# A spectral layer and a rational feed-forward block: a turn's transform task and row stage between TensorE's first and second product

## The chip, the cores and the metric

The kernel runs on one core of one Trainium2 chip. The metric is the device time of one execution in microseconds; the time of a kernel is the median of its runs. The engines of the core go through their own instruction streams, each in order, and wait for each other by semaphores: TensorE (PE; its weight loads are listed as PEld), VectorE (DVE), ScalarE (ACT), GpSimd (POOL) and SyncE (SP, which here only issues DMAs).

## The reference

```python
def _attn_ref(x, w_r, w_i, b_r, b_i):          # x: 4 x 3008 x 256
    X = np.fft.rfft(x, axis=1)
    Yr = Xr @ w_r - Xi @ w_i + b_r             # Xr, Xi: real and imaginary part of X
    Yi = Xr @ w_i + Xi @ w_r + b_i
    # soft threshold by 0.01 on both parts
    return np.fft.irfft(Yr + 1j * Yi, n=3008, axis=1)

def _moe_ref(x, w_in, w_out, a, b):            # x: 12032 x 256, w_in: 256 x 2048, w_out: 2048 x 256
    h = x @ w_in
    P = a[0] + a[1] * h + a[2] * h**2 + a[3] * h**3
    Q = 1.0 + abs(b[0]) * abs(h) + abs(b[1]) * h**2
    return (P / (Q + 1e-06)) @ w_out
```

The output of the first function, as 12032 rows, is the input of the second. All of it is float32.

## The kernel before

**Spectral part.** A transform of 3008 points is split in 47 x 64. An image (one of 4 batches) goes through tasks that are Python generators: `f1_task` (8 first-transform tasks, matmuls L195), `f2_task` (12, L255), `m_sum` and `m_rest` (12 each: the mix with w_r and w_i; L297 and L315), `i1_task` (12, the first inverse step, L376). Between them data turn around through DRAM. The tasks of image 0 run in a prologue, those of images 1 to 3 beside the feed-forward part, one or two per turn. The last inverse step is the row stage `i2_task` (L426), which makes the input xsh and xsl of one block of the feed-forward part.

**Feed-forward part.** The 12032 rows are cut in 26 blocks of 470 columns (two blocks have 376). A block goes through 8 units of 256 hidden columns, so there are 208 units. The main loop has one turn per unit i. In turn i TensorE computes the first product of unit i+1 (`g1_mm`, L460, 12 matmuls into the PSUM tile h) and the second product of unit i-3 (`g2_mm`, L553, 12 matmuls into acc). ScalarE reads h of unit i: v and s (L492, L493; step A), t (L499; step a), and for unit i-1 two activations on y (L504, step Y, and the reciprocal root L506, step y). A DMA from GpSimd's queue adds s to v (L497). VectorE computes t of unit i from h (L511, L512), then g of unit i-1 (L520, the high part; it waits for y), then whatever the turn's task left for it, then the low part of g of unit i-2 (L533), then v of unit i-1 (L523). GpSimd does one subtraction (L527). h has two PSUM buffers, so the first product of unit i+1 waits for VectorE's L512 of unit i-1. Blocks of work for the transform tasks take their PSUM from a second pair of buffers, `ft`.

**What sets the order.** The order of a turn is a string of steps, gone through letter by letter (L831):

```python
order = "Fs1AaehmYy2" if i < 4 else "F1AasYehmy2" if storing(i) else "Fs1AaYehmy2"
```

F lets the row stage (in two of eight turns) and the planned tasks issue their matmuls; for `m_sum` it first issues a copy of `offset` into the PSUM bank on ScalarE, `copy(0, pt[:, 0], offset)`, and the L297 matmuls wait for it. The steps 1 and 2 are the two products, s stores a finished block (two copies acc to ob on ScalarE), e and h let the tasks evict their PSUM on ScalarE (L159, L263, L264, L319, L429). VectorE's part of a task (L267, L268, L321, L437) comes after L520. Which tasks stand in which turn is set by a planner with fixed costs (`spent`, `budget`, `plan`), not by time. When no transform task is left (`nextb == B and not cur`), the string is changed: the row stage's second half comes late and another form of the stage is used. In that part of the program, from the turn after the last task, the order is the same in both kernels.

Of the kernel before, what the change touches and what calls it, by code (L numbers as in the profile page):

```python
# [18 lines left out]
B, S, D, DFF = 4, 3008, 256, 2048  # L19
# [82 lines left out]
def spectral_moe(ctx, tc, t, out):  # L102
# [61 lines left out]
    def flush():  # L164
        while late:
            late.pop(0)()
# [246 lines left out]
    def i2_task(n, ec):  # L413
        if ec == 0:
            alone[n] = nextb == B and not cur
            xs_t[n] = (mx.tile([128, 2, TB], F32R, tag="xsh", name="xsh"), mx.tile([128, 2, TB], F32R, tag="xsl", name="xsl"))
        xh, xl = xs_t[n]
        ct = c_t[n]
        w = len(blocks[n]) * TJ
        pt = ps.tile([128, 512], F32, tag="ft", name="pi2")  # L420
        last = len(blocks[n]) - 1
        for i in range(JB):
            z = slice(i * TJ, 512 if i == JB - 1 and not alone[n] else (i + 1) * TJ)
            if i <= last or not alone[n]:
                k = min(i, last)
                nc.tensor.matmul(out=pt[:, z], lhsT=ct[:, k, ec * 128:(ec + 1) * 128], rhs=i2[:, :z.stop - z.start],  # L426
                                 start=i == 0, stop=True, skip_group_check=True)
        yield
        nc.scalar.activation(out=xh[:, ec, :w], in_=pt[:, :w], func=ACTF.Copy)  # L429
        yield  # L430
        if alone[n]:
            nc.tensor.matmul(out=pt[:, :w], lhsT=minus, rhs=xh[:, ec, :w], start=False, stop=True, skip_group_check=True)
            yield
            nc.scalar.activation(out=xl[:, ec, :w], in_=pt[:, :w], func=ACTF.Copy)
        else:
            yield
            nc.vector.tensor_tensor(out=xl[:, ec, :w], in0=pt[:, :w], in1=v32(xh[:, ec, :w]), op=ALU.subtract)  # L437
# [48 lines left out]
    def act_a(u):  # L486
        w = width(u)
        d = un[u]
        h = d["h"][:, :, :w]
        for nm, bufs in (("s", 2), ("v", 4), ("t", 4)):  # L490
            d[nm] = fresh(nm, bufs, u)
        nc.scalar.activation(out=d["v"], in_=h, func=ACTF.Abs, scale=rate["b0"])  # L492
        nc.scalar.activation(out=d["s"], in_=h, func=ACTF.Square, scale=rate["b1"])  # L493
        if u < 2:
            nc.gpsimd.tensor_tensor(out=d["v"], in0=d["v"], in1=d["s"], op=ALU.add)
        else:
            nc.gpsimd.dma_start(out=d["v"], in_=d["s"], accum_op=ALU.add)  # L497
        yield
        nc.scalar.activation(out=d["t"], in_=h, func=ACTF.Identity, scale=rate["a3"], bias=ca[:, 2:3])  # L499

    def act_b(u):
        d = un[u]
        d["y"] = fresh("y", 3, u)
        nc.scalar.activation(out=d["y"], in_=d["v"], func=ACTF.Square, bias=C0)  # L504
        yield
        nc.scalar.activation(out=d["y"], in_=d["y"], func=ACTF.Abs_reciprocal_sqrt)  # L506
# [62 lines left out]
    def fft_tasks(b):  # L569
        turns = (0, 1, 2, 3, 6, 7, 4, 5) if b == 1 else range(8)  # L570
        ts = [(0.95, 2, 2, f1_task(b, c, pos), 0) for pos, c in enumerate(turns)]
        ts += [(0.0, 0, 0, load_first(b), 0)] + [(0.0, 0, 0, iter(()), 0)] * 2
        np_ = NK // 2
        for p in range(np_ + 2):
            if p < np_:
                ts.append((0.86, 1, 1, f2_task(b, p), 1))
            if p == 0:
                ts.append((0.0, 0, 0, iter(()), 0))
            if 1 <= p <= np_:
                ts += [(0.86, 1, 0, m_sum(b, p - 1), 2), (1.56, 0, 1, m_rest(b, p - 1), 0)]  # L580
            if p >= 2:
                ts.append((0.87, 1, 1, i1_task(b, p - 2), 0))
        return ts
# [29 lines left out]
    with tc.manual_schedule():  # L613
# [185 lines left out]
        cur = []  # L799
        nextb = 1  # L800
# [10 lines left out]
        storing = lambda i: i >= 4 and i % UB == 3  # L811
# [8 lines left out]
        for i in range(-1, nu + 4):  # L820
            flush()
            live = []
            parts = []
            freed = 0
            if i == 3:
                copied.append(1)
            if 0 <= i < nu:
                n, q = divmod(i, UB)
            aa = act_a(i) if 0 <= i < nu else iter(())
            ab = act_b(i - 1) if 0 <= i - 1 < nu else iter(())  # L830
            order = "Fs1AaehmYy2" if i < 4 else "F1AasYehmy2" if storing(i) else "Fs1AaYehmy2"  # L831
            for step in order.replace("m", "").replace("2", "2m").replace("1A", "Ao1") if nextb == B and not cur else order:
                if step == "F":
                    if 0 <= i < nu and n + 1 < nb and q in I2Q:
                        g = i2_task(n + 1, I2Q.index(q))
                        next(g)
                        parts.append(g)
                        held += 1
                        freed += 1
                    if not cur and nextb < B and i >= 0:  # L840
                        cur = first if nextb == 1 else fft_tasks(nextb)
                        last = max(next(k for k in range(nb) if blocks[k][-1] >= nextb * NJ) * UB - UB - 1, i + 1)
                        plan = [load(k) for k in range(i, last)]
                        level = (sum(x[0] for x in cur) + sum(plan)) / len(plan)
                        plan = [level - x for x in plan]
                        nextb += 1
                        spent = budget = 0.0
                    if cur:
                        budget += plan.pop(0) if plan else level
                        while cur and spent + cur[0][0] / 2 < budget and held + cur[0][1] <= 2 and not (live and storing(i)):  # L850
                            cost, use, free, g, part = cur.pop(0)
                            next(g, None)
                            (parts if part == 1 else live).append(g)
                            held += use
                            freed += free
                            spent += cost
                            if not cost or part == 2:
                                break
                elif step == "1" and i + 1 < nu:
                    g1_mm(i + 1)  # L860
                elif step == "2":
                    if 0 <= i - 3 < nu:
                        g2_mm(i - 3, (0, 1) if i - 3 >= UB else (1,))
                    if 0 <= i - 2 < UB:
                        g2_mm(i - 2, (0,))
                elif step == "s" and i >= 4 and (i - 4) % UB == UB - 1:
                    store((i - 4) // UB)
                elif step in "Aa":
                    next(aa, None)
                elif step == "o":  # L870
                    for g in owed:
                        drain(g)
                    owed = []
                elif step in "hm":
                    for g in parts:
                        next(g)
                elif step == "e":
                    for g in live:
                        next(g, None)
                    if i == 0:  # L880
                        next(mix)
                elif step in "Yy":
                    next(ab, None)
            prev, db = db, dve_b(i - 1) if 0 <= i - 1 < nu else iter(())
            next(prev, None)
            if 0 <= i < nu and alone.get(n + 1):
                owed, parts = parts, []
            if 0 <= i < nu:
                dve_a(i)
            if i == 0:  # L890
                drain(mix)
            next(prev, None)
            next(db, None)
            for g in live:
                drain(g)
            for g in parts:
                next(g, None)
            drain(prev)
            for g in parts:
                drain(g)  # L900
            next(db, None)
            if i >= nu:
                drain(db)
            held -= freed
            if len(cur) < 8 and 1 < nextb < B and (nextb, 0) not in xin:
                load_x(nextb, 0)
                load_x(nextb, 1)
            if 0 <= i < nu and q == 1 and n + 1 < nb:
                assert not cur or blocks[n + 1][-1] < (nextb - 1) * NJ
                load_c(n + 1)  # L910
# [33 lines left out]
```

## Time and profile before

| | |
|---|---|
| median of 3 runs | 1416.41 us (1415.95 to 1417.36) |
| profiled execution | 1419.05 us |
| its span, first to last instruction | 1417.3 us |
| granted TensorE clock, mean | 0.998 |
| TensorE matmul, weight loads | 98%, 85% of the span |
| VectorE, ScalarE, GpSimd | 91%, 81%, 47% |

Times in the rows below are microseconds from the start of the span. A matmul row is busy from its start to a modelled end, and matmuls are pipelined, so a busy TensorE may stand all the same: the distance between starts tells what a group of matmuls took. In a timeline each row has start, duration, engine, line, operation, output<-inputs, shape and count; in brackets stand the idle time of the engine just before it and what ended it.

### The profile page before, as it was taken

The page shows a single profiled execution, that of the slowest core. Times are in us where ns is not written, and L with a number is a line of the kernel's source. Part 1 is how long each engine was busy: PE and PEld are TensorE (multiplying, and loading weights), DVE is VectorE, ACT ScalarE, POOL GpSimd, SP SyncE. Part 2 cuts the span into 40 slices and gives each one's busy share as a digit, 9 for nine tenths or more (in the row PEclk, how much of TensorE's full clock was granted, in tenths as well). Part 3 has the DMA queues.
Part 4 walks back from the last instruction along what each step waited for, and adds up shares of the span by engine and source line. Part 5 has one row for each costly group of instructions (what it writes and reads, how often), then busy time and mean ns, then how long its engine had stood idle before and what let it go on. Part 6 is the DMA issues. An engine that isn't in the chain of part 4 may idle for free.

```text
span 1417.3 us, 20378 instructions
## 1 busy us (share of the span) xinstructions
PE 1390.0 (98%) x7279; PEld 1210.9 (85%) x7279; DVE 1291.5 (91%) x1304; ACT 1144.5 (81%) x1513; POOL 670.5 (47%) x444
## 2 busy tenths in 40 slices
PE   9998999999999999999999999999999999999997
PEld 4977889998878989898888899998888888888887
DVE  3779899898999989999989999999999999999998
ACT  2768887887888778888888778888888898888985
POOL 0444444444554444454545444444545555555553
PEclk9999999999999999999999999999999999999999
DMA  9966556556776556556687465656555465555543
GB/s 309 379 215 162 117 121 150 110 114 158 160 204 151 116 130 141 117 121 156 148 208 158 98 142 126 127 115 133 108 127 118 97 122 96 112 118 99 117 77 80
DMA packets 95657, 200.48 MB, mean 141 GB/s; under 512 B 10748, under 2 KB 51748, under 8 KB 95556
## 3 DMA queue, kind: packets, MB, share of 16 engines
q0 software_dynamic: 29664, 97.62, 38.0%
q1 hardware_dynamic: 65780, 101.51, 23.2%
q8 instruction: 58, 0.95, 0.3%
q14 instruction: 43, 0.35, 0.1%
q10 hardware_dynamic: 112, 0.05, 0.0%
HBM read 54.61 MB, written 37.49 MB: 65 GB/s over the span
## 4 chain that ended last, share of the span: by engine, by line
PE 72%; DVE 10%; issue 9%; ACT 5%; DMA 4%; SPq 0%; DVEq 0%; ACTq 0%
PE h L460 28%; PE acc L553 27%; PE pi L426 4%; PE pft L315 4%; DVE t L511 3%; DVE v L523 3%; PE pft L376 2%; DMA v<-s 2%; PE pft L297 2%; PE pft L255 2%; PE pft L195 1%; PE pft L178 1%; DVE g L520 1%; ACT t L499 1%; DMA s<-zt 1%
## 5 line engine op out<-in xcount | busy, mean ns | idle before, releaser
L553 PE MATMUL acc<-g,wsp 128*128 128x470 f32 (+1 forms) x2496 | 563.7, 375 | 3.4 <-DVE g L533 3.4
L527 POOL TENSOR_TENSOR t<-t,v 128x940 f32<-128x940 f32 (+1 forms) x206 | 469.7, 2280 | 164.4 <-DVE v L523 143.8
L553 PEld LDWEIGHTS acc<-g,wsp 128*128 128x128 f32 x2496 | 470.0, 190 | 62.8 <-DVE g L533 5.0
L460 PE MATMUL h<-xsh,win 128*128 128x470 f32 (+1 forms) x1664 | 436.9, 384 | 6.0 <-DVE t L512 5.6
L497 POOL DMA_DIRECT2D v<-s x206 | 181.6, 882 | 489.7 <-issue 452.9
L460 PEld LDWEIGHTS h<-xsh,win 128*128 128x128 f32 x1664 | 304.8, 189 | 61.6 <-PE acc L553 9.8
L520 DVE SCALAR_TENSOR_TENSOR g<-t,small,y 128x940 fp32r<-128x940 f32 (+1 forms) x208 | 250.3, 1203 | 45.8 <-ACT y L506 42.6
L492 ACT ACTIVATE v<-h 128x940 f32<-128x940 f32 (+1 forms) x208 | 196.2, 943 | 95.4 <-PE h L460 92.1
L511 DVE TENSOR_TENSOR t<-t,h 128x940 f32<-128x940 f32 (+1 forms) x208 | 231.3, 1112 | 27.3 <-ACT t L499 25.6
L512 DVE SCALAR_TENSOR_TENSOR t<-t,small,h 128x940 f32<-128x940 f32 (+1 forms) x208 | 245.2, 1179 | 7.4
L533 DVE SCALAR_TENSOR_TENSOR g<-t,small,y 128x940 fp32r<-128x940 f32 (+1 forms) x208 | 244.2, 1174 | 0.1
L460 PE MATMUL h<-xsl,win 128*128 128x470 f32 (+1 forms) x832 | 241.4, 371 | 0.0
L523 DVE SCALAR_TENSOR_TENSOR v<-v,g 128x940 f32<-128x940 f32 (+1 forms) x208 | 231.8, 1114 | 0.1
L504 ACT ACTIVATE y<-v 128x940 f32<-128x940 f32 (+1 forms) x208 | 206.1, 991 | 21.4 <-DMA v<-s 21.4
L499 ACT ACTIVATE t<-h,small 128x940 f32<-128x940 f32 (+1 forms) x208 | 216.2, 1039 | 0.0
L506 ACT ACTIVATE y<-y 128x940 f32<-128x940 f32 (+1 forms) x208 | 205.1, 986 | 2.0
L493 ACT ACTIVATE s<-h 128x940 f32<-128x940 f32 (+1 forms) x208 | 195.7, 941 | 0.0
L460 PEld LDWEIGHTS h<-xsl,win 128*128 128x128 f32 x832 | 155.8, 188 | 20.1
L426 PEld LDWEIGHTS pi<-small,ct 96*128 96x128 f32 x516 | 65.2, 192 | 7.9 <-ACT s L493 3.6
L426 PE MATMUL pi<-small,ct 96*128 96x94 f32 (+1 forms) x516 | 66.2, 275 | 3.5 <-DVE x L268 2.9
L159 ACT ACTIVATE pft<-offset 128x256 f32<-128x256 f32 x36 | 14.1, 391 | 57.6 <-DVE yt L321 23.3
L255 PEld LDWEIGHTS pft<-f,bt 128*128 128x128 f32 x288 | 37.3, 191 | 4.9 <-DVE yt L321 1.9
(113 smaller groups left out, 1071.0 us busy)
## 6 DMA issues: line engine op xcount, KB each, us to landing
v<-s POOLq DMA_DIRECT2D x190, 470.0 KB, 4.7
xin<-in_x SPq DMA_DIRECT2D x30, 512.0 KB, 6.4
s<-zt SPq DMA_DIRECT2D x48, 256.0 KB, 3.5
out_t<-ob SPq DMA_DIRECT2D x48, 235.0 KB, 4.5
ct<-s SPq DMA_DIRECT2D x20, 480.0 KB, 5.6
bt<-s SPq DMA_DIRECT2D x36, 256.0 KB, 3.3
y<-yt SPq DMA_DIRECT2D x144, 64.0 KB, 2.3
s<-a SPq DMA_DIRECT2D x46, 192.0 KB, 5.1
```

Source lines behind the costliest of these rows:

```text
L460: nc.tensor.matmul(out=h[:, i, :w], lhsT=l, rhs=r, start=k == 0, stop=k == len(halves) // FU - 1)
L492: nc.scalar.activation(out=d["v"], in_=h, func=ACTF.Abs, scale=rate["b0"])
L499: nc.scalar.activation(out=d["t"], in_=h, func=ACTF.Identity, scale=rate["a3"], bias=ca[:, 2:3])
L504: nc.scalar.activation(out=d["y"], in_=d["v"], func=ACTF.Square, bias=C0)
L506: nc.scalar.activation(out=d["y"], in_=d["y"], func=ACTF.Abs_reciprocal_sqrt)
L511: nc.vector.tensor_tensor(out=tt, in0=tt, in1=h, op=ALU.mult)
L512: nc.vector.scalar_tensor_tensor(out=tt, in0=tt, scalar=ca[:, 1:2], in1=h, op0=ALU.add, op1=ALU.mult)
L520: stt(out=hi, in0=tt, scalar=ca[:, 0:1], in1=y, op0=ALU.add, op1=ALU.mult)
L523: stt(out=v, in0=v, scalar=C0, in1=v32(hi), op0=ALU.add, op1=ALU.mult)
L527: nc.gpsimd.tensor_tensor(out=tt[:, :cut], in0=tt[:, :cut], in1=v[:, :cut], op=ALU.subtract)
L533: stt(out=lo, in0=tt, scalar=ca[:, 0:1], in1=y, op0=ALU.add, op1=ALU.mult)
L553: nc.tensor.matmul(out=acc[n][e][:, :w], lhsT=l, rhs=r, start=begun[n][e] == 1, stop=begun[n][e] == 3 * FU * UB)
```

## The change

The branch for the time without transform tasks becomes explicit, with the same strings as before. In the other branch, from turn 4 on, F comes behind 1, A and a (and behind the store's s where there is one to store: `1AaFs`).

```diff
-            order = "Fs1AaehmYy2" if i < 4 else "F1AasYehmy2" if storing(i) else "Fs1AaYehmy2"
-            for step in order.replace("m", "").replace("2", "2m").replace("1A", "Ao1") if nextb == B and not cur else order:
+            if nextb == B and not cur:
+                order = "FAo1asYehy2m" if storing(i) else "FsAo1aYehy2m"
+            else:
+                order = "Fs1AaehmYy2" if i < 4 else "1AaFsYehmy2" if storing(i) else "s1AaFYehmy2"
+            for step in order:
```

TensorE, a turn beside the transforms of the first image there; L255 is an f2 task, L460 the first product, L553 the second (before):

```order
L553 MATMUL acc_1256<-g,wsp_774 128x470 x4
L255 MATMUL pft<-f_70,bt 128x2x64 x4
L460 MATMUL h<-xsh,win_594 128x470 x4
L460 MATMUL h<-xsl,win_594 128x470 x2
L460 MATMUL h<-xsh,win_594 128x470 x4
L460 MATMUL h<-xsl,win_594 128x470 x2
L553 MATMUL acc_1255<-g,wsp_774 128x470 x2
```

and the same place now:

```order
L553 MATMUL acc_1256<-g,wsp_774 128x470 x4
L460 MATMUL h<-xsh,win_594 128x470 x4
L460 MATMUL h<-xsl,win_594 128x470 x2
L460 MATMUL h<-xsh,win_594 128x470 x4
L460 MATMUL h<-xsl,win_594 128x470 x2
L255 MATMUL pft<-f_70,bt 128x2x64 x4
L553 MATMUL acc_1255<-g,wsp_774 128x470 x2
```

The task's matmuls have moved over the 12 matmuls of the first product and stand right before the second.

ScalarE, a turn with `m_sum` (the row `pft<-offset` is the offset copy, `pft<-pft` the eviction step of `m_sum`; before):

```order
L506 ACTIVATE y<-y 128x940
L159 ACTIVATE pft<-offset 128x256
L492 ACTIVATE v<-h 128x940
L493 ACTIVATE s<-h 128x940
L499 ACTIVATE t<-h,small 128x940
L504 ACTIVATE y<-v 128x940
L159 ACTIVATE pft<-pft 128x256
L506 ACTIVATE y<-y 128x940
```

and now:

```order
L506 ACTIVATE y<-y 128x940
L492 ACTIVATE v<-h 128x940
L493 ACTIVATE s<-h 128x940
L499 ACTIVATE t<-h,small 128x940
L159 ACTIVATE pft<-offset 128x256
L504 ACTIVATE y<-v 128x940
L159 ACTIVATE pft<-pft 128x256
L506 ACTIVATE y<-y 128x940
```

The offset copy has moved behind t; the evictions of the tasks stay where they were, in front of L506.

TensorE, the last turn with a transform task (a row stage L426 and an i1 task L376) and the first turn without, whose own row stage is the second L426 (before):

```order
L553 MATMUL acc_9424<-g,wsp_774 128x470 x2
L426 MATMUL pi_9502<-small,ct 128x94 x4
L426 MATMUL pi_9502<-small,ct 128x136
L376 MATMUL pft<-y,g_71 128x256 x2
L460 MATMUL h<-xsh,win_621 128x470 x4
L460 MATMUL h<-xsl,win_621 128x470 x2
L460 MATMUL h<-xsh,win_621 128x470 x4
L460 MATMUL h<-xsl,win_621 128x470 x2
L553 MATMUL acc_9423<-g,wsp_801 128x470 x4
```

and now:

```order
L553 MATMUL acc_9424<-g,wsp_774 128x470 x2
L460 MATMUL h<-xsh,win_621 128x470 x4
L460 MATMUL h<-xsl,win_621 128x470 x2
L460 MATMUL h<-xsh,win_621 128x470 x4
L460 MATMUL h<-xsl,win_621 128x470 x2
L426 MATMUL pi_9522<-small,ct 128x94 x4
L426 MATMUL pi_9522<-small,ct 128x136
L376 MATMUL pft<-y,g_71 128x256 x2
L553 MATMUL acc_9423<-g,wsp_801 128x470 x4
```

Row stage and task now follow the first product of that turn; the next turn's row stage still precedes its first product. VectorE's, GpSimd's and SyncE's instructions stand in the same order in both kernels.

## Rows read from the trace of the kernel before

**Rows 1.** Windows: stretch and length; busy us (count) by engine, clock, DMA.

```profile
core 0: us, PE busy (x) PEld busy (x) DVE busy (x) ACT busy (x) POOL busy (x), PEclk, DMA share, GB/s
143.00:1045.00 902.00, 895.54 (x4749) 791.71 (x4748) 827.60 (x820) 740.85 (x995) 421.97 (x273) 1.00 0.62 137
1045.00:1400.00 355.00, 351.62 (x1719) 309.47 (x1719) 351.51 (x325) 312.47 (x371) 198.59 (x131) 1.00 0.54 107
```

**Rows 2.** Waits, 143 to 1045 us: who <- for whom: total, times, longest.

```profile
ACT v L492 <- PE h L460: 62.5, 80, 1.3
DVE g L520 <- ACT y L506: 41.6, 58, 3.5
DVE t L511 <- ACT t L499: 24.5, 33, 1.1
ACT pft L159 <- DVE yt L321: 23.3, 12, 2.4
```

**Rows 3.** Timeline, a turn with an f2 task and `m_sum`.

```profile
805.00 1.20 PE L460 MATMUL h<-xsh,win 128*128 128x470 f32 x4
...
808.74 0.39 ACT L159 ACTIVATE pft<-offset 128x256 f32<-128x256 f32 x1 [1.87 <-DVE yt L321]
...
811.20 1.03 PE L297 MATMUL pft<-wr,total 128*128 128x256 f32 x4
...
811.88 1.21 PE L460 MATMUL h<-xsh,win 128*128 128x470 f32 x4
...
812.53 0.39 ACT L159 ACTIVATE pft<-pft 128x256 f32<-128x256 f32 x1
812.84 0.39 ACT L263 ACTIVATE total<-pft 128x256 f32<-128x256 f32 x1
...
813.57 1.01 ACT L506 ACTIVATE y<-y 128x940 f32<-128x940 f32 x1
...
814.61 1.20 DVE L520 SCALAR_TENSOR_TENSOR g<-t,small,y 128x940 fp32r<-128x940 f32 x1 [0.45 <-ACT y L506]
...
815.73 0.41 DVE L267 TENSOR_TENSOR total<-pft,total 128x256 f32<-128x256 f32 x1
...
816.66 1.19 DVE L533 SCALAR_TENSOR_TENSOR g<-t,small,y 128x940 fp32r<-128x940 f32 x1
```

**Rows 4.** Timeline, turns without a task: TensorE, then VectorE from one v to the next.

```profile
1050.32 1.02 PE L460 MATMUL h<-xsh,win 128*128 128x470 f32 x4
...
1052.90 2.72 PE L553 MATMUL acc<-g,wsp 128*128 128x470 f32 x12
...
1055.46 1.02 PE L460 MATMUL h<-xsh,win 128*128 128x470 f32 x4
...
1061.15 1.13 DVE L523 SCALAR_TENSOR_TENSOR v<-v,g 128x940 f32<-128x940 f32 x1
...
1066.69 1.13 DVE L523 SCALAR_TENSOR_TENSOR v<-v,g 128x940 f32<-128x940 f32 x1
```

**Rows 5.** Timeline, a turn with row stage and mixed product: its end, evictions, VectorE's part.

```profile
784.53 1.01 PE L460 MATMUL h<-xsh,win 128*128 128x470 f32 x4
784.73 0.60 ACT L319 ACTIVATE yt<-pft 128x512 f32<-128x512 f32 x1 [1.87 <-PE pft L315]
...
785.23 0.56 ACT L429 ACTIVATE xsh<-pi 128x470 fp32r<-128x470 f32 x1
...
785.67 0.99 ACT L506 ACTIVATE y<-y 128x940 f32<-128x940 f32 x1
...
787.81 0.68 DVE L321 SCALAR_TENSOR_TENSOR yt<-pft,yt 128x512 f32<-128x512 f32 x1
...
788.41 0.64 DVE L437 TENSOR_TENSOR xsl<-pi,xsh 128x470 fp32r<-128x470 f32 x1
```

**Rows 6.** Timeline, the same turn on TensorE: first product before it, and its row stage.

```profile
774.67 1.21 PE L460 MATMUL h<-xsh,win 128*128 128x470 f32 x4
...
781.79 1.36 PE L426 MATMUL pi<-small,ct 96*128 96x94 f32 x10 [1.61 <-DVE x L268]
```

**Rows 7.** Timeline, the last turn with a transform task.

```profile
1036.95 1.29 PE L426 MATMUL pi<-small,ct 96*128 96x94 f32 x10
...
1038.76 1.20 PE L460 MATMUL h<-xsh,win 128*128 128x470 f32 x4
...
1041.10 1.20 DVE L520 SCALAR_TENSOR_TENSOR g<-t,small,y 128x940 fp32r<-128x940 f32 x1 [1.34 <-ACT y L506]
```

## The prediction

> **What bounds the kernel now.** I read the busy sums by stretch first, then the waits, then one turn as a timeline. From 143 to 1045 us, the stretch beside transforms, two engines are nearly full: TensorE's matmul rows cover 895.5 of 902 us and VectorE's 827.6 (ScalarE's 740.9), at a granted clock of 1.00, the 2.4 GHz level. From 1045 us on, with no transforms left, VectorE is busy 351.5 of 355 us and nothing else matters [rows 1]. A busy TensorE row can hide a stall, so I went by starts. In a turn without a task the first product starts at 1050.32 us, the second at 1052.90 and the next first product at 1055.46: 2.58 + 2.56 = 5.14 us for 24 matmuls [rows 4]. The turn with an f2 task and a "sum" task lasts from 805.00 to 811.88 = 6.88 us, and the two tasks alone account for the 1.74 us over 5.14 [rows 3]. Turns of the same make-up repeat that length, so beside transforms TensorE issues without pause and sets the pace, except in six places named below. VectorE and ScalarE wait there for each other: 24.5 us for t, 23.3 us of ScalarE's offset copy for VectorE [rows 2]. In one turn the offset copy waited 1.87 us at the head of ScalarE's queue [rows 3], with v, s and t behind it. None of that is TensorE time.
>
> **The change, part by part.** No instruction is added or removed; VectorE's, GpSimd's and SyncE's order stays, and the step that moves issues no DMA. (a) ScalarE: the offset copy (0.39 us) goes behind v, s and t. The matmul that waits for it now comes after a whole first product, so the copy has time; t comes earlier. On TensorE's path this is worth 0. Its cover: VectorE is done with the bank's old contents 2.05 us after it starts g (814.61 to 816.66 [rows 3]), and v, s and t, each longer than the 0.60 us of a narrower eviction [rows 5], stand in front. Without that cover the copy would hold up y and not v: up to the 1.87 us of today's wait, in that turn alone. (b) TensorE: a turn's tasks come after the first product of the next unit. The sum of matmuls is the same. What changes is when the results of a task are there compared with the first products: later by one first product plus the task's own length, 2.58 + 1.74 = 4.3 us in the turn of [rows 3]. ScalarE's order is unchanged at that point: it evicts the task's results and only then makes y by the reciprocal root, and VectorE's g waits for y. Before, ScalarE reached the eviction when the task was just done (812.53 us against 811.88). Now it will stand and wait for TensorE, with y queued behind, and for y waits VectorE's whole remaining turn, up to the t that frees the bank for the first product but one.
>
> So I write down that new loop. From the start of one first product: 2.58 us of it, the task, 0.20 us until ScalarE starts (784.53 to 784.73 [rows 5]), ScalarE's evictions E, 1.04 us from y to VectorE's g (813.57 to 814.61 [rows 3]), VectorE's turn of 5.54 us (1061.15 to 1066.69 [rows 4]) with its part D of the task's results, and some 0.2 us back to TensorE (an estimate, as the hand-over just named). In the same time TensorE goes through two turns: 2 x 5.14 us, this task and the next turn's. A task costs a turn 0.16 us more than its matmuls take, for the switch of products. The task itself cancels. TensorE stalls by E + D - 0.88 - (what the next turn's task adds), if that is above 0.
>
> The sizes. f2 and sum: E = 1.04 (812.53 to 813.57), D = 0.93 (815.73 to 816.66). f2 alone: E = 0.73 (812.84 to 813.57), D = 0.93. A four-matmul product alone: 0.68 us (811.20 to 811.88), some 0.7 added to a turn [rows 3]. Mixed product: E = 0.50, D = 0.60; row stage: E = 0.44, D about 0.55 (its 0.64 less the overlap) [rows 5]. First transform: two evictions like the mixed product's, E = 1.0, D = 0 (an estimate).
>
> Most turns pass. After f2 and sum comes the mixed product, which adds 1.7 us or more: 1.97 - 0.88 - 1.7 is below 0. The first transforms one after another (1.0 - 0.88 - 1.2) pass too. Where a heavy task is followed by a light turn or none, they don't:
> - f2 and sum, then no task: 1.97 - 0.88 = 1.09 us. Three such places; one lies in the narrow block (some 0.8), one where a second product is narrow and TensorE short (some 1.5). Sum 3.4.
> - row stage and f2, then a short product: 0.73 + 1.48 - 0.88 - 0.7 = 0.6, twice: 1.2.
> - row stage and mixed product, then a short product: 0.94 + 1.15 - 0.88 - 0.7 = 0.5, once.
> - a first transform, then two turns without a task: over two turns VectorE adds 2 x (5.54 - 5.14) less once, so 1.0 - 0.88 + 0.40 = 0.5, twice: 1.0.
> - an inverse product with f2, then a short product: some 0.1, four times: 0.4.
> That is 6.5 us of new stalls in 12 places.
>
> What goes: six places where TensorE stands today because a task comes too early for the PSUM bank it needs. One is the row stage at 781.79 us, which waited for VectorE's x; that turn lasts from 774.67 to 784.53 = 9.86 us, 1.9 more than the shortest of its make-up [rows 5, 6]. Against the shortest turn of the same make-up the six lose 2.5, 0.95, 1.3, 1.6, 1.0 and 1.95 us. A task that comes 2.6 us later finds the bank free. The first I walked through: there the next first product itself has to wait for VectorE, and 1.3 of the 2.5 us come back. Sum: 8.1 us. What is late next there is VectorE, as in the list above.
>
> The tail. From 1045 us on VectorE is full, so the end stands as far behind VectorE's last wait as now. That wait ends at 1041.10 us with the y behind the last transform task; its turn began with the task at 1036.95, and the task (1.81 us) ended at 1038.76 [rows 7]. In the new order the same turn begins with the first product, 2.6 us, and the task, its evictions, y and g follow later by that. It costs 2.6 us; from 2.2, if a pause of VectorE's in the tail takes some of it, to 2.6.
>
> Sum: 6.5 + 2.6 - 8.1 = +1.0 us. The profiled execution took 1419.05 us (span 1417.3 and 1.75 around it) and would take 1420.1; it lies 2.6 us above the median of the runs, 1416.41, so the median should come to 1417.4. What a measurement of this kernel can tell from no change is about 0.2%, 2.8 us: I forecast no difference that can be told. Bounds: each of the 12 places hangs on hand-overs that I know to 0.2 us or so, which makes 2.4 us either way; the stalls that go, from 5 us (every place is replaced in part, as the first) to 9.3 (all of it). With the tail's bounds that is -3.0 to +6.5 us. The ends won't all meet, and 1414 to 1420 is the forecast's own range.
>
> One rule speaks for another reading. [Rows 1] show 791.7 us of weight loads in the 902, 88%, and VectorE at 92%. The Trainium skill (Perfetto Trace Analysis, section Identifying the Most-Contended Engine) says that the busy share of the matmul row is a bad measure and that of the weight loads is to be taken; by it VectorE, not TensorE, is the most contended engine beside transforms too. The trace agrees only in part: the starts of the matmuls show no gap for VectorE to fill.
>
> **Rivals.** (1) Faster: the tasks come late enough and the new loop has more slack than I give it. For it: VectorE waited only 41.6 us for y in 902 [rows 2], and ScalarE is busy 82% of the stretch. Against: y's queue position is fixed by the order. Then all 8.1 us come back and only the tail's 2.6 are paid: 1416.4 - 5.5 = 1410.9. (2) Slower: the new wait, ScalarE's evictions for TensorE with y behind, takes more. Mechanism and place are those of the 12 places. For it: already today ScalarE stood 1.87 us before an eviction whose product came late, with y behind [rows 5], and VectorE at 92% can't catch up. Each 0.1 us on the loop costs 1.2 us; from 0.15 us more per hand-over chain it decides (1.0 + 1.8 = 2.8). At 0.5 us more, with the next pairs also over the line, it gives +7: 1423.4. (3) VectorE is the bound beside transforms, so its 24.5 us of waiting for t, which the offset copy causes, come off the time: 1392. For it the shares above; against it the even turn lengths on TensorE. (4) The order does nothing: TensorE's sum is the same and neither stalls nor tail move: 1416.4. Against it: the tail's shift follows from two orders that don't depend on timing.
>
> **How the numbers follow.** Forecast 0.45, of which most lies within 0.2% and a tenth beyond on the slow side. Rival 1: 0.18. Rival 2: 0.27. Rival 3: 0.03. Rival 4: 0.07. Faster: rivals 1 and 3, 0.21. Slower: rival 2 and some of the forecast, 0.33. Same: the rest, 0.46. The range reaches to rivals 1 and 2: 1411 to 1424, with the forecast's own inside.
>
> **What would show it.** In the profile after: waits of ScalarE on v for h fall far below 62.5 us and turn up on the evictions (yt, zt, total, the copy of half a bank, a) for TensorE, several times as much as now; the offset copy's waits for VectorE go; VectorE waits more for y and less for t. The row stage's wait for x and its like go from TensorE, and TensorE waits for t (bank of h) before first products in the turns without a task. VectorE's last long wait before the tail ends some 2 to 4 us later. The forecast is wrong where TensorE's turns in steady stretches get longer everywhere, not only in the 12 places, or where VectorE enters the tail earlier than now.

## The result and the profile after

| | kernel before | changed kernel |
|---|---|---|
| median | 1416.88 us (1415.93 to 1418.2, 6 runs) | 1426.95 us (1425.22 to 1427.91, 6 runs) |
| ratio | | 1.0069, 95% interval 1.0056 to 1.0082 |
| profiled execution, span | 1419.05, 1417.3 us | 1425.22, 1423.4 us |

The change made the kernel slower by 0.7%, about 10 us, more than the 0.2% that can be told. The forecast was 1417.4 us, no difference that can be told, with a range of 1411 to 1424. So it was wrong: the time lies outside the range, and the loss is clear. Rival 2 (slower, the new wait takes more) was priced at 1423.4.

The same two windows as in [rows 1], changed kernel:

```profile
143.00:1045.00 902.00, 893.84 (x4708) 782.05 (x4708) 815.44 (x813) 729.11 (x982) 414.54 (x271) 1.00 0.61 136
1045.00:1400.00 355.00, 350.98 (x1708) 306.83 (x1707) 349.92 (x323) 312.45 (x370) 195.77 (x129) 1.00 0.54 108
```

In the same 902 us every engine does less. The clock is 1.00, the 2.4 GHz level, as before. TensorE's matmul row hides most of the loss (895.5 to 893.8); 41 matmuls fewer show it better.

The waits of 143 to 1045 us, as in [rows 2]:

```profile
DVE g L520 <- ACT y L506: 79.3, 84, 1.9
ACT yt L319 <- PE pft L315: 52.6, 33, 3.0
ACT pft L159 <- PE pft L297: 43.0, 35, 2.3
ACT zt L159 <- PE pft L376: 29.7, 34, 2.2
...
PEld h L460 <- DVE xsl L437: 7.6, 13, 1.2
...
PE h L460 <- DVE t L512: 4.0, 7, 0.8
PEld h L460 <- DVE t L512: 3.7, 9, 0.8
...
PE h L460 <- DVE xsl L437: 3.0, 4, 0.8
```

Much of this was foreseen: ScalarE stands before the evictions for TensorE, and VectorE waits for y (41.6 to 79.3 us). No step of the prediction has the first product waiting for xsl.

**Where the 10 us lie.** In both orders the same matmuls have been done when a given second product starts, so those starts can be compared one by one. The first of the main loop, the one behind the last transform task, and one near the end; kernel before, then changed kernel:

```profile
118.12 1.23 PE L553 MATMUL acc<-g,wsp 128*128 128x470 f32 x5
...
1047.73 2.75 PE L553 MATMUL acc<-g,wsp 128*128 128x470 f32 x12
...
1396.93 3.60 PE L553 MATMUL acc<-g,wsp 128*128 128x376 f32 x20
```

```profile
115.39 1.86 PE L553 MATMUL acc<-g,wsp 128*128 128x470 f32 x8
...
1051.66 1.67 PE L553 MATMUL acc<-g,wsp 128*128 128x470 f32 x7
...
1403.10 1.20 PE L553 MATMUL acc<-g,wsp 128*128 128x376 f32 x6
```

From first to second row it takes 929.61 us before and 936.27 now: +6.66. From there to the third 349.20 and 351.44: +2.24. The sum of 8.9 us is the effect as the profiles show it. (The loop's own start lies between 114.8 and 118.1 us over the profiled executions of all kernels here.) Going through the second products between, the difference moves in steps. A step is read at the second product of the turn named; a turn has the number i of its unit:

| place | steps, us | prediction |
|---|---|---|
| six old bank stalls of the list (turns 5 and 6, 14, 34, 53, 60, 101) | -7.6 | -8.1 |
| a seventh old bank stall (turn 12) | -0.7 | not in the list |
| first product of a new block, waiting for xsl (turns 7, 15, 23, 31, 39, 55, 63, 79, 87, 103) | +5.4 | +0.5 at turn 79's place, by another wait |
| row stage and f2, then a short product (turns 56, 104) | +0.8 | +1.2 |
| f2 and sum, then no task (turns 114 to 116, 123 and 124, 131 and 132) | +5.05 | +3.4 |
| last first transforms, then two empty turns (turns 49 to 51, 97 to 99) | +1.1 | +1.0 |
| heavy turns with a short turn behind them just after the start (turns 9, 11) | +1.2 | not in the list |
| small steps at other turns | +1.4 | +0.4 |
| tail | +2.2 | +2.6 |

**An old stall that went.** TensorE, the turn of [rows 6]:

```profile
779.72 1.02 PE L460 MATMUL h<-xsh,win 128*128 128x470 f32 x4
...
782.30 1.29 PE L426 MATMUL pi<-small,ct 96*128 96x94 f32 x10
...
787.54 0.81 PE L460 MATMUL h<-xsh,win 128*128 128x470 f32 x3
```

The row stage no longer waits; the turn takes 7.82 us in place of 9.86.

**The missed wait.** A block's input is xsh and xsl; its second row stage now ends just one second product ahead of the block's first product. All three engines, changed kernel:

```profile
253.35 1.29 PE L426 MATMUL pi<-small,ct 96*128 96x94 f32 x10
...
256.23 0.60 ACT L319 ACTIVATE yt<-pft 128x512 f32<-128x512 f32 x1 [2.59 <-PE pft L315]
256.72 0.56 ACT L429 ACTIVATE xsh<-pi 128x470 fp32r<-128x470 f32 x1
257.17 0.99 ACT L506 ACTIVATE y<-y 128x940 f32<-128x940 f32 x1
...
258.19 1.20 DVE L520 SCALAR_TENSOR_TENSOR g<-t,small,y 128x940 fp32r<-128x940 f32 x1 [1.84 <-ACT y L506]
258.61 1.02 PE L460 MATMUL h<-xsh,win 128*128 128x470 f32 x4
...
259.90 0.64 DVE L437 TENSOR_TENSOR xsl<-pi,xsh 128x470 fp32r<-128x470 f32 x1
...
260.60 0.48 PE L460 MATMUL h<-xsl,win 128*128 128x470 f32 x1 [0.76 <-DVE xsl L437]
```

Read it from top to bottom. ScalarE stands 2.59 us for the mixed product of the same turn, evicts it and xsh, and then makes y. VectorE stands 1.84 us for y; xsl, whose input was there at 257.3, comes behind g and yt. The first product starts on xsh, reaches xsl and stops.

**A task turn ahead of a turn without a task:**

```profile
920.36 0.37 ACT L159 ACTIVATE pft<-pft 128x256 f32<-128x256 f32 x1 [1.11 <-PE pft L297]
...
921.38 1.00 ACT L506 ACTIVATE y<-y 128x940 f32<-128x940 f32 x1
...
922.21 1.02 PE L460 MATMUL h<-xsh,win 128*128 128x470 f32 x4
...
922.42 1.20 DVE L520 SCALAR_TENSOR_TENSOR g<-t,small,y 128x940 fp32r<-128x940 f32 x1 [1.44 <-ACT y L506]
...
925.43 2.85 PE L553 MATMUL acc<-g,wsp 128*128 128x470 f32 x12 [0.50 <-ACT ob L159]
...
929.12 1.10 PE L460 MATMUL h<-xsh,win 128*128 128x470 f32 x4 [0.84 <-DVE t L512]
```

The loop is the predicted one: task late, evictions late, y behind them, g, and at last t, for which the first product stands 0.84 us. The store's copy of acc on ScalarE is late as well and holds the second product by 0.50. The prediction hadn't got that one. Of the 5.05 us of these three places, 3.1 lie at the first product that waits for t, 1.5 at the second product that waits for the copy, and 0.46 already in turn 114, whose own first product waits for t.

**The tail**, answering [rows 7]:

```profile
1040.83 1.03 PE L460 MATMUL h<-xsh,win 128*128 128x470 f32 x4
...
1044.52 1.03 PE L376 MATMUL pft<-y,g 128*128 128x256 f32 x4
...
1047.55 1.20 DVE L520 SCALAR_TENSOR_TENSOR g<-t,small,y 128x940 fp32r<-128x940 f32 x1 [1.81 <-ACT y L506]
```

Last turn's start to VectorE's last wait: 6.72 us, before 4.15; that is 2.57 more. 2.2 reach the end.

### The profile page after: what moved, and what is told of

The parts are those of the page before. It is cut to its first block, busy times and chain, and to the rows that moved or that the text cites. A ratio compares the mean times of both kernels' runs of the same rounds, so it can differ in the third digit from the quotient of the medians.

```text
span 1423.4 us, 20162 instructions
## 1 busy us (share of the span) xinstructions
PE 1395.7 (98%) x7279; PEld 1206.9 (85%) x7279; DVE 1286.6 (90%) x1304; ACT 1142.3 (80%) x1513; POOL 666.9 (47%) x444
## 4 chain that ended last, share of the span: by engine, by line
PE 69%; DVE 15%; issue 10%; ACT 4%; DMA 2%; DVEq 0%; SPq 0%; ACTq 0%
PE h L460 27%; PE acc L553 24%; DVE t L511 4%; DVE v L523 4%; PE pi L426 4%; PE pft L315 4%; PE pft L255 3%; PE pft L376 2%; PE pft L297 2%; DVE t L512 2%; DVE g L533 1%; PE pft L195 1%; DVE g L520 1%; PE pft L178 1%; ACT y L506 1%
## 5 line engine op out<-in xcount | busy, mean ns | idle before, releaser
L553 PE MATMUL acc<-g,wsp 128*128 128x470 f32 (+1 forms) x2496 | 579.8, 381 | 4.0 <-DVE g L533 3.4
L527 POOL TENSOR_TENSOR t<-t,v 128x940 f32<-128x940 f32 (+1 forms) x206 | 451.0, 2189 | 254.8 <-DVE v L523 229.7
L553 PEld LDWEIGHTS acc<-g,wsp 128*128 128x128 f32 x2496 | 464.6, 190 | 74.7 <-issue 11.4
L460 PE MATMUL h<-xsh,win 128*128 128x470 f32 (+1 forms) x1664 | 423.7, 376 | 11.8 <-DVE t L512 10.6
L460 PEld LDWEIGHTS h<-xsh,win 128*128 128x128 f32 x1664 | 307.4, 189 | 64.9 <-PE acc L553 13.5
L520 DVE SCALAR_TENSOR_TENSOR g<-t,small,y 128x940 fp32r<-128x940 f32 (+1 forms) x208 | 246.8, 1187 | 84.7 <-ACT y L506 82.3
L512 DVE SCALAR_TENSOR_TENSOR t<-t,small,h 128x940 f32<-128x940 f32 (+1 forms) x208 | 245.2, 1179 | 7.4
L460 PE MATMUL h<-xsl,win 128*128 128x470 f32 (+1 forms) x832 | 244.3, 373 | 3.1 <-DVE xsl L437 3.0
L533 DVE SCALAR_TENSOR_TENSOR g<-t,small,y 128x940 fp32r<-128x940 f32 (+1 forms) x208 | 244.5, 1176 | 0.1
L506 ACT ACTIVATE y<-y 128x940 f32<-128x940 f32 (+1 forms) x208 | 203.4, 978 | 2.0
L460 PEld LDWEIGHTS h<-xsl,win 128*128 128x128 f32 x832 | 155.7, 188 | 28.5 <-DVE xsl L437 8.0
L426 PEld LDWEIGHTS pi<-small,ct 96*128 96x128 f32 x516 | 65.5, 192 | 3.0 <-issue 0.8
L426 PE MATMUL pi<-small,ct 96*128 96x94 f32 (+1 forms) x516 | 65.9, 275 | 0.0
L319 ACT ACTIVATE yt<-pft 128x512 f32<-128x512 f32 x36 | 21.6, 599 | 52.6 <-PE pft L315 52.6
L159 ACT ACTIVATE zt<-pft 128x512 f32<-128x512 f32 x47 | 27.9, 596 | 32.0 <-PE pft L376 31.8
```

The source lines that it names most:

```text
L460: nc.tensor.matmul(out=h[:, i, :w], lhsT=l, rhs=r, start=k == 0, stop=k == len(halves) // FU - 1)
L512: nc.vector.scalar_tensor_tensor(out=tt, in0=tt, scalar=ca[:, 1:2], in1=h, op0=ALU.add, op1=ALU.mult)
L520: stt(out=hi, in0=tt, scalar=ca[:, 0:1], in1=y, op0=ALU.add, op1=ALU.mult)
L527: nc.gpsimd.tensor_tensor(out=tt[:, :cut], in0=tt[:, :cut], in1=v[:, :cut], op=ALU.subtract)
L533: stt(out=lo, in0=tt, scalar=ca[:, 0:1], in1=y, op0=ALU.add, op1=ALU.mult)
L553: nc.tensor.matmul(out=acc[n][e][:, :w], lhsT=l, rhs=r, start=begun[n][e] == 1, stop=begun[n][e] == 3 * FU * UB)
```

## The experiments

After reading the two traces, theory 1 was: the forecast's loop is right, and the missing term is xsl. Theory 2: everything on the loop is later and the places are symptoms. Differences below are between ratios to the kernel before, times 1416.4 us. Each ratio is known to about 0.0010 to 0.0014, so a difference of two of them to some 2 to 3 us.

**xsl ahead of g** (`low` holds the row stage's generators; VectorE alone):

```diff
+            for g in low:
+                next(g, None)
             next(db, None)
```

> The changed kernel with one edit: on VectorE the low part of a row stage (xsl, 0.64 us) stands ahead of the turn's g and no longer behind it. TensorE's order is that of the changed kernel. Theory 1: the missing term is the wait of a new block's first product for xsl (about 6.2 us over some 14 blocks, 1 to 1.6 us each on the profile's weight-load and matmul rows). xsl then runs in the time in which VectorE waits for y anyway, so g loses little: 1427 - 6.2 = about 1421, and the waits for xsl of line 460 go from the trace (20 of them, 11.8 us, to under 2 us). Theory 2 (the loop of evictions, y and g is longer everywhere by some 0.5 us; xsl is late only because VectorE is late): the lateness stays and moves to the bank wait (t) or behind g: within 2 us of 1427. Also possible: g is held up by xsl, each of 28 row stages costs up to 0.64 us, then 1427 or more.

Measured: 1418.40 us, 1.0014 (1.0004 to 1.0024): 7.8 us less than the changed kernel. The same place:

```profile
256.67 0.65 DVE L437 TENSOR_TENSOR xsl<-pi,xsh 128x470 fp32r<-128x470 f32 x1 [1.52 <-ACT xsh L429]
...
257.54 1.20 DVE L520 SCALAR_TENSOR_TENSOR g<-t,small,y 128x940 fp32r<-128x940 f32 x1 [0.23 <-ACT y L506]
...
257.97 1.02 PE L460 MATMUL h<-xsh,win 128*128 128x470 f32 x4
...
258.83 0.59 PE L460 MATMUL h<-xsl,win 128*128 128x470 f32 x2
```

xsl stands in the time in which VectorE waits for y, g loses nothing, and no wait for xsl is left on TensorE. Theory 1 holds: its 6.2 us, and some more.

**The same edit on the kernel before:**

> The kernel before with the same edit on VectorE (xsl ahead of g), as the control of the run above. There the row stage stands ahead of the first product and xsl is early enough anyway. Theory 1: no block's first product waits for xsl, so nothing to gain: 1416.9 within 1.5 us; a few tenths may be lost where g is held up. Theory 2 gives the same here; a gain of over 3 us would say that xsl's place matters for another reason than the new order, and the reading of the run above falls.

Measured: 1414.93 us, 0.9994 (0.9984 to 1.0004): no difference that can be told. So it is the new order that made xsl's place cost something. The profiled execution was the shortest of its twelve (1412.34); the old bank stalls there are smaller by 0.3 to 1.3 us at five places (turns 5, 12, 14, 34, 101), and the median doesn't show that as a gain. The main loop of that execution is 3.9 us shorter than in the profile of the kernel before, more than the interval of the ratio allows (2.3 us): sizes read from one execution can carry an error of a microsecond or two in sum.

**Old order in the last transform turn alone:**

```diff
+                if i == 141:
+                    order = "F1AasYehmy2" if storing(i) else "Fs1AaYehmy2"
```

> The changed kernel, in which only the turn with the last inverse transform (turn 141, the last before the tail) has the old order: row stage and transform task ahead of the first product. Prediction's tail term: VectorE enters the tail 2.2 to 2.6 us earlier: 1427 - 2.4 = 1424.6. Rival: the tail is filled from its own end (VectorE has slack there, or another wait ends last): no change, 1427.

Measured: 1424.14 us, 1.0056 (1.0043 to 1.0069). The intervals overlap, so the times alone don't settle it. In the profile the part behind the last transform task takes 349.31 us (before 349.20, changed kernel 351.44): the tail's term is there, 2.1 us.

**Old order ahead of turns without a task** (as above, with `i in (48, 96, 114, 122, 130)`):

> The changed kernel, in which five turns have the old order: the last of the first transforms ahead of two turns without a task (turns 48 and 96) and the turns with an f2 and a sum task ahead of a turn without a task (114, 122, 130). Theory 1 (with the sizes read from the two traces): 1.1 us come back at the first two, 5.0 us at the other three, 6.1 in all: about 1421. By the sizes of the prediction (0.5 each and 3.4) it would be 4.4: 1422.6. Theory 2 (everything is later, the places don't matter): under 2 us, and the stall moves to the next turns.

Measured: 1420.73 us, 1.0038 (1.0025 to 1.0051): 4.4 us by the ratios, 6.2 by the medians; the sizes from the trace said 6.1. The ratios alone leave theory 2 nearly possible; in the profile the main loop takes 931.28 us in place of 936.27, 5.0 less, all of it at the places named. The place matters, as theory 1 has it.

**The three edits together:**

> The changed kernel with the three edits of the runs before together: xsl ahead of g on VectorE, old order in turns 48, 96, 114, 122 and 130, and old order in turn 141. If the three causes are separate, the ratios add: 1.0069 - 0.0055 - 0.0031 - 0.0013 = 0.997, about 1412, below the kernel before; what is left of the change is then its gain at the old bank stalls (about 8 us) less the small steps of 0.1 to 0.6 us between other pairs of turns. Rival: the edits cover one another (one lateness of VectorE seen at three places): 1416 to 1418.

Measured: 1412.80 us, 0.9974 (0.9963 to 0.9985), where the sum of the single ratios was 0.997. So the three losses add and don't cover one another, and the mended kernel beats the kernel before. Whether they have one cause behind them this run can't tell.

**Part (a) undone, offset copy again ahead of v, s and t** (its step P comes in front: `"P1AaFsYehmy2"`, `"Ps1AaFYehmy2"`):

> The changed kernel with only part (a) undone: the offset copy stands again ahead of v, s and t on ScalarE, TensorE's order is the new one. The prediction put part (a) at nothing on TensorE's path: within 1.5 us of 1427. Rival: with the tasks later, VectorE is done with the copy's bank later than in the kernel before, the copy holds up v, s and t by 1 to 2.5 us in each of 36 turns with a sum task, and where the next first product then waits for t, TensorE stands 0.2 us or more: 1434 or more. Third: the copy in front keeps ScalarE from waiting later, and gains 1 to 2 us.

Measured: 1425.90 us, 1.0073 (1.0059 to 1.0086). Part (a) is worth nothing that can be told, as predicted, but the cover is another one than I named. All that is left of the 53.5 us for which the copy waited for VectorE before (23.3 of it in [rows 2]):

```profile
ACT pft L159 <- DVE xsl L438: 5.5, 3, 1.8
...
ACT pft L159 <- DVE yt L322: 1.9, 1, 1.9
```

(Lines are one higher here.) ScalarE, held up by its evictions, comes to the copy when VectorE has long left the bank: over the 35 copies from 143 to 1045 us it left it 4.7 us before the copy on the median, where before the copy started right behind it.

**New order only in the eight turns where a task stood for its bank before**, old order elsewhere:

```diff
+                if i >= 4 and not (i in (5, 6, 12, 14, 34, 53, 60, 101)):
+                    order = "F1AasYehmy2" if storing(i) else "Fs1AaYehmy2"
```

> New order only in eight turns (5, 6, 12, 14, 34, 53, 60, 101), those in which a task of the kernel before stood for its bank; the old order in all the others, with the offset copy behind v, s and t throughout. Theory 1: the bank stalls go (7 to 8 us) and none of the new waits comes: about 1409. Rival: the turn after, whose tasks stand at the old place, then comes 2.6 us too early for its banks, and the stall moves there: 1414 to 1417. If the offset copy behind v, s and t hurts the old order (a sum's matmuls wait for it with TensorE's first product behind), it is slower than 1417 by up to 36 times some tenths.

Measured: 1415.76 us, 0.9996 (0.9987 to 1.0005). My first theory missed here and the rival held: most of the stall moves one turn on.

```profile
200.93 2.73 PE L553 MATMUL acc<-g,wsp 128*128 128x470 f32 x12
...
204.21 0.68 DVE L321 SCALAR_TENSOR_TENSOR yt<-pft,yt 128x512 f32<-128x512 f32 x1
...
204.94 1.13 PE L376 MATMUL pft<-y,g 128*128 128x256 f32 x4 [1.28 <-DVE yt L321]
```

Turn 14's task stands late, turn 15's early: they now lie only one second product apart, and VectorE is still reading the bank.

**The same with xsl ahead of g:**

> The run above with xsl ahead of g. In the kernel before this edit was worth -0.9 us (interval -2.3 to +0.6). Theory 1: no block's first product waits for xsl in the old order, so within 1.5 us of the run above. Rival: row stages free their banks earlier, which takes off what is left of the bank stalls: 1 to 3 us below it.

Measured: 1411.91 us, 0.9965 (0.9952 to 0.9979): 4.4 us below the run above, more than even the rival gave. The waits of a task for its bank fall from 5.0 us on the matmul rows to 1.5. VectorE's xsl reads the row stage's bank, and earlier xsl frees it sooner. Theory 1 had no such gain.

**y ahead of the evictions, from turn 4 on** (ScalarE alone; TensorE's and VectorE's orders are those of the changed kernel):

```diff
-"1AaFsYehmy2" if storing(i) else "s1AaFYehmy2"
+"1AaFsYyehm2" if storing(i) else "s1AaFYyehm2"
```

> The changed kernel with one edit on ScalarE alone: from turn 4 on, the y by the reciprocal root stands ahead of the evictions of the turn's task results and no longer behind them. TensorE's and VectorE's orders are those of the changed kernel. Theory 1 (y behind evictions that wait for TensorE is the hinge of all the new stalls): y fits into the time in which ScalarE stands for TensorE (162 us in the trace of the changed kernel), VectorE's g starts earlier, the waits for xsl go as well (VectorE is done with g sooner; 6 us), so do most of the stalls ahead of empty turns (5 to 6 us), the start (1.5 us) and part of the tail (up to 2 us): about 1412 to 1415, and VectorE's wait of g for y falls from 79 us to under 45. Theory 2 (y is only the messenger; what is late is the task's results): evictions come 1.04 us later in each turn, the banks and xsl with them, and the next v: 1425 to 1432, with more waits of TensorE for xsl.

Measured: 1408.59 us, 0.9946 (0.9932 to 0.9960): 17.4 us below the changed kernel and more than theory 1 gave. Window and waits:

```profile
143.00:1045.00 902.00, 902.00 (x4786) 799.04 (x4786) 844.51 (x828) 757.04 (x999) 423.54 (x275) 1.00 0.62 139
```

```profile
ACT yt L319 <- PE pft L315: 36.6, 29, 2.7
...
DVE t L511 <- ACT t L499: 11.8, 28, 0.7
...
DVE g L520 <- ACT y L506: 8.4, 10, 3.0
```

From 143 to 1045 us TensorE has no wait for xsl, for t or for a bank in its list any more; from turn 12 on, turns of one make-up in wide blocks agree within 0.1 us from first product to first product, and the main loop takes 920.10 us (before 929.61, changed 936.27), the part behind it 349.72 (349.20, 351.44). VectorE's wait for y is 8.4 us in place of 79.3. ScalarE still stands for the evictions (36.6 in place of 52.6 for yt), and what is behind them now, v, s and t of the next turn, holds up VectorE in places (11.8 us for t, none in the changed kernel), but TensorE nowhere. So xsl's lateness was the same cause at one remove: xsl is behind g, g waits for y, y is behind the evictions.

**The same in the five turns alone** (48, 96, 114, 122, 130):

> The same edit in the five turns 48, 96, 114, 122 and 130 alone (a task turn ahead of turns without a task). By the prediction's sum of the loop (stall = E + D - 0.88) the evictions' E leaves it there: for f2 and sum 0.93 - 0.88 = 0.05 is left, for the last first transforms nothing. So the 6.2 us that the old order in these five turns gave come back here too, with the task still behind the first product: about 1421. If the place of the task itself is the cause (its results late), and not y's place in ScalarE's queue, 1425 to 1427 stay.

Measured: 1420.96 us, 1.0029 (1.0017 to 1.0041): the same as the old order in these turns (1.0038, intervals overlap), with the tasks still late. The place shown above, in this run:

```profile
917.49 0.99 ACT L506 ACTIVATE y<-y 128x940 f32<-128x940 f32 x1
...
918.57 0.37 ACT L159 ACTIVATE pft<-pft 128x256 f32<-128x256 f32 x1
...
920.42 1.02 PE L460 MATMUL h<-xsh,win 128*128 128x470 f32 x4
...
925.80 1.10 PE L460 MATMUL h<-xsh,win 128*128 128x470 f32 x4
```

The turn without a task takes 5.38 us in place of 6.91. At these places it is y's place in ScalarE's queue, not the task's place on TensorE.

**y ahead in the kernel before:**

> The kernel before with the edit that took the changed kernel to 1408.6 us (y ahead of the evictions on ScalarE, from turn 4 on, up to the last transform). TensorE's order is that of before, tasks ahead of the first product. Theory 1 (the old order's stalls are tasks that come too early for their banks, and y has no part in them): y ahead holds up the evictions by 1.04 us, the banks come free later, nothing is gained: 1417 to 1421. Then the change is worth some 8 us once y stands ahead. Rival: y ahead is a gain by itself, because VectorE is earlier in every turn and with it the banks: 1409 to 1412, and the changed order gains nothing of its own.

Measured: 1414.27 us, 0.9983 (0.9974 to 0.9992): a gain of 2.4 us, where theory 1 had none and the rival 5 or more. Both are half right. Earlier y lets VectorE leave the banks sooner, but the tasks still come too early; what is left of TensorE's waits for a bank:

```profile
PE pi L426 <- DVE x L268: 2.3, 2, 1.2
...
PE pi L426 <- DVE xsl L437: 0.6, 1, 0.6
...
PE pft L255 <- DVE yt L321: 0.5, 1, 0.5
```

With y ahead in both, the change is worth 0.9983 - 0.9946, about 5 us, as a gain.

**y ahead, with the offset copy in front:**

> The changed kernel with y ahead, and with the offset copy again ahead of v, s and t. With y behind the evictions the place of the copy made no difference (ratio 1.0073 against 1.0069). Theory: it makes none here either, since TensorE nowhere stands in the kernel with y ahead and VectorE is done with the bank earlier still: 1408.6 within 1.5 us. Rival: with ScalarE no longer standing for TensorE late in the turn, the copy reaches its bank before VectorE has left it, holds up v, s and t again (waits of the copy for VectorE as in the kernel before, 57 us in all) and costs 2 us or more.

Measured: 1407.50 us, 0.9937 (0.9923 to 0.9950), not told apart from 0.9946. The copy waited for VectorE 1.0 us in all. Part (a) does nothing that can be told in either setting.

## Why the prediction was wrong

- **Old stalls, right, in part by luck.** The six places gave -7.6 us against -8.1 (the six sizes listed make 9.3, less 1.3 that come back: 8.0). A seventh place, turn 12 of the kernel before, was not in the list and gave 0.7 more; together -8.3. There, at 183.84 us, an f2 task stood for VectorE (waits of the kernel before, 143 to 1045 us):

```profile
PE pft L255 <- DVE yt L321: 1.5, 1, 1.5
```

- **Part (a), right in size.** Nothing that can be told, in two settings; the cover was ScalarE's own lateness.
- **The new loop, right in mechanism.** ScalarE's evictions for TensorE, y behind them, g, t, bank: the rows show it, and y ahead in five turns takes it away. For the first transforms 1.1 us against 1.0.
- **The step that failed: "Most turns pass."** The list followed y to one end only, the bank of h. VectorE's late turn also ends in xsl, which a block's first product needs at once. This wait is 5.4 us in the trace at ten places, and 7.8 by the run that moves xsl (7.7 in its profile: 5.7 at these ten places, 0.6 in the tail, the rest at other turns). The list had three of the places, under the bank's wait: at two, row stage and f2 (turns 55 and 103), both waits came, xsl first and the bank one turn on (0.8 against 1.2); at the third, row stage and mixed product (turn 79), xsl came in its place. So the forecast lacked 4.9 us.
- **A wrong sum: row stage and f2.** E was put at 0.73, f2's alone; with the row stage's 0.44 it is 1.17, and the place comes to 1.07 us, 2.1 for the two. Found at the bank: 0.42 each. The smaller sum was nearer, without a reason.
- **A term mis-sized: f2 and sum, then no task.** 3.4 predicted, 5.05 found. The loop was summed for the first product alone, and there it holds (3.1, and 0.46 in turn 114); ScalarE's late copy of acc holds a second product as well, 1.5 us.
- **A term left out of the list:** two heavy turns with a short turn behind them just after the start, 1.2 us by the trace. The formula covers the first (1.2 for a mixed product with f2, then a short product; 0.64 found at turn 9). At turn 11 (0.54) TensorE is short because turn 10 has 4 matmuls of the second product in place of 12. With the missed wait (+4.9), the two sizes (-0.4 and +1.65) and this term the forecast's +1.0 becomes +8.4, of the 8.9 in the two profiles.
- **The tail, right:** 2.57 to VectorE's last wait, 2.2 at the end, against 2.2 to 2.6.
- **Rivals.** 1 and 4 (faster, nothing) are out by the time. Rival 2's mechanism is what happened, but its price, more time on the same 12 places, missed the other consumer. Rival 3 (VectorE's waits for t come off) fell: they went (24.5 us to none in the list of waits) and the kernel got slower. In the kernel with y ahead the weight loads cover 799.0 of 902 us, 89%, and VectorE 844.5, 94%; TensorE's matmul rows have no wait in that stretch, and the turn lengths are its own sums. By the rule of the Trainium skill cited in the prediction (Perfetto Trace Analysis, section Identifying the Most-Contended Engine) VectorE would still be the one to work on. The trace disagrees there.

How a wait spreads fits another sentence of the Trainium skill (Perfetto Trace Analysis, section Tensor Engine Instruction (MATMUL, LD_WEIGHTS)), that ScalarE, VectorE and GpSimd take their instructions strictly first in, first out. The trace agrees at 256.23 us: y needed nothing of the mixed product, and stood behind its eviction, for which ScalarE waited 2.59 us.

The small steps at other turns (+1.4 us) were not taken apart one by one; they go with y ahead, no more is shown.

## What to carry to other kernels

Where a producer is moved later, list everything that stands behind its consumers in their queues, and follow each to all who wait for it, not to the first. A wait costs by what is queued behind it: ScalarE stood 163 us before evictions with y behind; with y ahead it still stood 128 us there, but TensorE lost nothing by it, and the kernel was 17.4 us shorter. If a reordering loses where it was to gain, first try the order on the engine that now waits; here that one edit turned +0.7% into -0.5%.

## What was not expected of the hardware

The same VectorE instruction has two lengths. The group of g (L520), 143 to 1045 us: changed kernel, then kernel before with y ahead (the last figure ahead of the second bar is the mean in ns):

```profile
L520 DVE SCALAR_TENSOR_TENSOR g<-t,small,y 128x940 fp32r<-128x940 f32 (+1 forms) x135 | 160.6, 1189 | 81.8 <-ACT y L506 79.3 <-PE acc L553 1.7
```

```profile
L520 DVE SCALAR_TENSOR_TENSOR g<-t,small,y 128x940 fp32r<-128x940 f32 (+1 forms) x137 | 190.4, 1390 | 7.9 <-ACT y L506 6.3 <-PE h L460 1.5
```

Most single rows of 940 columns take 1.19 or 1.20 us; of the others many take 1.5 us and more, the rest lie between. In four kernels (before and changed, each with y behind and ahead), the short ones lie beside GpSimd's subtraction (L527) for 0.03 to 0.10 us on the mean, those of 1.45 us and more for 0.5, and L527 was still running when each of these began. L527's own mean goes from 2.19 us in the changed kernel to 2.42 where most g are long. So y ahead lets g start earlier, in part beside L527, and those g are the longer ones: 137 x 0.20 = 27 us of VectorE in the kernel before with y ahead. That L527 is the cause is not shown. To lie beside it is not enough: L512, the same operation on as many columns, lies beside L527 for 0.8 us or more of its length in all four kernels and takes 1.19 to 1.20 us, no longer than L533, which never does. L512 reads h out of PSUM where g reads y; whether that decides, no run tells. The longer g may be why y ahead gained only 2.4 us there; no run separates it. In the kernel with y ahead and the new order the mean is 1288 ns, and part of VectorE's 94% is this.

The clock stayed at 1.00 in all the windows shown.
